# Attention rows and router logits from one matmul, the slot table entered two chunks after places, 16 instead of 40 warming matmuls

## The chip, the cores and the metric

One NeuronCore of a Trainium2 chip runs the whole program. The metric is the device time of one launch in microseconds (us). Matmuls run on TensorE (PE), with the load of their stationary operand shown apart as PEld; VectorE is DVE, ScalarE is ACT, GpSimd is POOL, and SyncE (SP) only starts DMAs here. Each engine takes its own instructions strictly in the written order and waits on semaphores for the others.

## The reference

Eight batches of 576 tokens pass three layers, all in float32. B=8, H=8, S=576, D=64, E=8.

```python
scores = q @ k.T / sqrt(64)              # per batch and head
ret = scores * where(i >= j, gamma[h] ** (i - j), 0)
x = (ret @ v)                            # 4608 tokens x 512
logits = x @ w_gate                      # 512 x 8
expert = argmax(logits)
gate = softmax(logits)[expert]
x = gate * (relu(x @ w1[expert]) @ w2[expert])     # 512 -> 1024 -> 512
h = x @ w_in                             # 512 -> 2048
out = (h * cos(h)) @ w_out               # 2048 -> 512
```

## The kernel before

The program has three stages, one after the other: attention with routing (0 to about 285 us in the profile), the experts (to 759 us, where the dense layer's first matmul starts) and the dense layer. The change lies in the first and at the seam to the second.

**Attention.** A batch's 576 tokens are five chunks of 128, 128, 128, 128 and 64; with eight batches that makes 40 chunks, and the loop over `i` runs 45 steps. Causal attention with decay is done as a recurrence: within a chunk by a masked score matrix (`scores`, `intra`), from earlier chunks by a 64x64 state per head that is kept in PSUM (tile `S`, copied to `sbd`) and multiplied with the queries (`inter`). A step holds pieces of several chunks: transposes of q and k of chunk i+1, scores of chunk i, output of chunk i-1, and the routing work of chunks i-2 and i-3. The schedule is written by hand: the order of the calls in the loop is the order on each engine, and no scheduler moves anything.

**Names.** `xt` holds a chunk's attention output with features on partitions; `rows` transposes it (tile `tp`) so that tokens lie on partitions, copies it to `xs` on ACT and stores it to `xd` in device memory, from where the experts later gather rows. `logits` multiplies `xt` by the router's weights (`wgp`, padded to 32 columns) into four 32-partition strips of `lg`; ACT copies them to `lt`; `logits_out` sums the strips and turns them over with a second matmul; DVE copies the eight logits of each token to `lgt`.

**Routing.** When a batch's logits are there, `route` finds the argmax (DVE), and `place` counts tokens before each one (short bf16 matmuls into `lg`) and works out each token's slot: a chain of some 15 small DVE instructions, one POOL instruction that DVE waits for, and more POOL instructions (`oh`, `rt`) behind it. `table` then enters token numbers and gates into the slot table with a matmul from `oh` and `rt`, and DVE adds the result to `tab`. Seven batches are placed as groups of five chunks; the last is split in groups of 2, 1 and 2 chunks, so that little is left at the end. After the last group `sid` (which row to gather for each slot) starts the gather DMAs of the first expert.

**PSUM.** There are eight banks of 128 x 512 float32. The attention stage uses two each for `tp`, `sc` (scores) and `x`, and one each for `S` and `lg`.

**The seam.** While the first gather runs, 40 bf16 matmuls whose result nobody reads are issued (`warm`, L189), so that PE is not idle. Behind them in PE's order stand the transposes of the first gathered rows (L602), which wait for the gate multiplication on ACT (L592), and then the experts' first layer (L620).

Of the kernel before, what the change touches and what calls it, by code (L numbers as in the profile page):

```python
# [11 lines left out]
F32 = mybir.dt.float32  # L12
# [5 lines left out]
ALU = mybir.AluOpType  # L18
AX = mybir.AxisListType
# [3 lines left out]
P = 128  # L23
# [3 lines left out]
E = 8  # L27
# [3 lines left out]
CH = [(0, 128), (128, 128), (256, 128), (384, 128), (512, 64)]  # L31
# [6 lines left out]
IDC = 2304  # L38
MAXOVB = 40
NWARM = 28  # L40
NWARM2 = 40
NWARM3 = 40

INV2PI = 1.0 / (2.0 * math.pi)
# [16 lines left out]
C_EYE = C_BASE + E  # L61
# [42 lines left out]
def attn_moe_kernel(ctx, tc, q, k, v, wg, w1, w2, win, wout, ctab, out):  # L104
    nc = tc.nc
# [3 lines left out]
    mm = nc.tensor.matmul  # L109
# [17 lines left out]
    ident = ct[:, C_ID:C_ID + 128]  # L127
# [54 lines left out]
    def w_units(e):  # L182
        return [(0, e, 0), (0, e, 1), (1, e, 0), (1, e, 1)]
# [8 lines left out]
    with ExitStack() as actx:  # L192
        ap1 = actx.enter_context(tc.tile_pool(name="ap1", bufs=1))
        ap2 = actx.enter_context(tc.tile_pool(name="ap2", bufs=2))
        ap3 = actx.enter_context(tc.tile_pool(name="ap3", bufs=3))
        ps2 = actx.enter_context(tc.tile_pool(name="ps2", bufs=2, space=PSUM))
        ps1 = actx.enter_context(tc.tile_pool(name="ps1", bufs=1, space=PSUM))
# [3 lines left out]
        def cc(col, n, rows=P):  # L201
            return ca[:rows, col - C_MASK:col - C_MASK + n]
# [4 lines left out]
        rsb = ap1.tile([P, E], BF16, name="rsb")  # L207
        rbase = ap1.tile([P, E], BF16, name="rbase")
        wgs = ap1.tile([P, 4, E], F32, name="wgs")
        wgp = ap1.tile([P, 4, 32], F32, name="wgp")  # L210
        nc.gpsimd.memset(wgp, 0.0)

        gx = ap1.tile([P, NCH, 4, P], F32, name="gx")
        tab = ap1.tile([P, 3, SL], F32, name="tab")
# [2 lines left out]
        def setup():  # L217
            nc.vector.tensor_copy(out=tri, in_=cc(C_TRI, P))
            nc.vector.tensor_copy(out=ones, in_=cc(C_ONE, P))
            nc.vector.tensor_copy(out=rbase, in_=cc(C_BASE, E))  # L220
            nc.vector.memset(rsb, 0.0)
            nc.vector.tensor_copy(out=wgp[:, :, 0:E], in_=wgs)

        def decay_table(c):
            for j in range(4):
# [3 lines left out]
        xts = []  # L229
        for i in range(3):  # L230
            t = ap1.tile([P, 4, P], F32, name=f"xt{i}")
# [3 lines left out]
        for i in range(2):  # L235
            t = ap1.tile([P, 4, P], F32, name=f"sbd{i}")
            nc.gpsimd.memset(t, 0.0)
            sbd.append(t)
        lgt = []
        for i in range(2):  # L240
            t = ap1.tile([P, NCH, E], F32, name=f"lgt{i}")
# [3 lines left out]
        steps = [(b, c) for b in range(B) for c in range(NCH)]  # L245
        NS = len(steps)
        st = [dict() for _ in steps]
# [35 lines left out]
        def scores(i):  # L283
            b, c = steps[i]
            o, n = CH[c]
            s = st[i]
            pT = ap2.tile([P, H, P], F32, tag="pT", name="pT")
            scs = [ps2.tile([P, 4, P], F32, tag="sc", name="sc") for g in range(2)]
            for a in range(4):
                for g in range(2):  # L290
                    r = 64 * g
                    mm(out=scs[g][:n, a, :n], lhsT=s["kpT"][r:r + 64, a, :n], rhs=s["qT"][r:r + 64, a, :n],
                       start=(a == 0), stop=True, skip_group_check=True)
            m = mask[:n, :n].unsqueeze(1).to_broadcast([n, 4, n])
            for g in range(2):
                nc.vector.tensor_mul(out=pT[:n, g::2, :n], in0=scs[g][:n, :, :n], in1=m)
            s["pT"] = pT
# [34 lines left out]
        def rows(i):  # L332
            b, c = steps[i]
            o, n = CH[c]
            pt = ps2.tile([P, 4, P], F32, tag="tp", name="tp")
            for j in range(4):
                nc.tensor.transpose(pt[:, j, :], xts[i % 3][:, j, :], ident)
            x = ap3.tile([P, 4, P], F32, tag="xs", name="xs")
            nc.scalar.copy(out=x[:n], in_=pt[:n])
            nc.sync.dma_start(out=xd[b * SEQ + o:b * SEQ + o + n, :], in_=x[:n].rearrange("p j t -> p (j t)"))  # L340

        def logits(i):
            b, c = steps[i]
            o, n = CH[c]
            s = st[i]
            x = xts[i % 3]
            lp = ps1.tile([P, 512], F32, tag="lg", name="lg")
            for j in range(4):
                mm(out=lp[32 * j:32 * j + 32, :n], lhsT=wgp[:, j, :], rhs=x[:, j, :n], start=True, stop=True,
                   skip_group_check=True)  # L350
            lt = ap2.tile([P, P], F32, tag="lt", name="lt")
            nc.scalar.copy(out=lt[:, :n], in_=lp[:, :n])
            s["lp"], s["lt"] = lp, lt

        def logits_out(i):
            b, c = steps[i]
            o, n = CH[c]
            s = st[i]
            lp, lt = s["lp"], s["lt"]
            mm(out=lp[:n, 256:256 + E], lhsT=lt[:, :n], rhs=cc(C_EYE, E), start=True, stop=True,  # L360
               skip_group_check=True)
            nc.vector.tensor_copy(out=lgt[b % 2][:n, c, :], in_=lp[:n, 256:256 + E])

        def cst(col, c0, n):
            return cc(col + c0 * E, n * E).rearrange("p (c e) -> p c e", e=E)
# [1 line left out]
        def route(i0, n):  # L367

            b, c0 = steps[i0]
            L = lgt[b % 2][:, c0:c0 + n, :]  # L370
            sh = [P, n, E]
            mx = ap2.tile([P, n], F32, tag="mx", name="mx")
            nc.vector.tensor_reduce(out=mx, in_=L, axis=AX.X, op=ALU.max)
            df = ap2.tile(sh, F32, tag="df", name="df", bufs=3)
            nc.vector.tensor_sub(out=df, in0=L, in1=mx.unsqueeze(2).to_broadcast(sh))
            sc = ap2.tile(sh, F32, tag="rsc", name="rsc")
            nc.vector.scalar_tensor_tensor(out=sc, in0=df, scalar=0.0, in1=cst(C_REV, c0, n), op0=ALU.is_ge,
                                           op1=ALU.mult)
            m2 = ap2.tile([P, n], F32, tag="m2", name="m2")
            nc.vector.tensor_reduce(out=m2, in_=sc, axis=AX.X, op=ALU.max)  # L380
            ohb = ap2.tile(sh, BF16, tag="ohb", name="ohb", bufs=3)
            nc.vector.tensor_tensor(out=ohb, in0=sc, in1=m2.unsqueeze(2).to_broadcast(sh), op=ALU.is_equal)
            routed.append((i0, n, ohb, df))
# [82 lines left out]
        def table(enter, gates):  # L466
            if gates is None:
                tp = enter(0, 3)
                nc.vector.tensor_add(out=tab, in0=tab, in1=tp)
                return  # L470
            tp = enter(0, 1)

            nc.vector.scalar_tensor_tensor(out=sid, in0=tab[:, 0, :], scalar=float(IDC), in1=tp[:, 0, :], op0=ALU.add,
                                           op1=ALU.add)
            gates()
            tp = enter(1, 3)
            nc.vector.tensor_add(out=tab[:, 1:3], in0=tab[:, 1:3], in1=tp)
            nc.vector.tensor_add(out=sgate, in0=tab[:, 1, :], in1=tab[:, 2, :])


        groups = {b * NCH + NCH - 1: (b * NCH, NCH) for b in range(B - 1)}
# [3 lines left out]
        routed = []  # L485
        tabled = []
# [20 lines left out]
        transposes(0)  # L507
        decay_k(1)
        wq = [(key, g) for key in w_units(0) for g in range(2)]
        for i in range(NS + 5):  # L510
            if i + 1 < NS:
                transposes(i + 1)
            if 0 <= i - 3 < NS:
                logits_out(i - 3)
            if i - 3 in groups:
                route(*groups[i - 3])
            if 0 <= i - 2 < NS:
                rows(i - 2)
            if i < NS:
                scores(i)  # L520
            if i + 2 < NS:
                decay_k(i + 2)
            if 20 <= i < 20 + len(wq):
                unit_split(*wq[i - 20], upA)
            if i == 0:
                setup()
            if 1 <= i <= NS:
                inter(i - 1)
                intra(i - 1)
            prev, tabled[:] = tabled[:], []  # L530
            for r in prev:
                table(*r)
            prev, routed[:] = routed[:], []
            for r in prev:
                place(*r)
            if 0 <= i - 2 < NS:
                logits(i - 2)
            if i + 4 < NS:
                loads(i + 4)
            if 18 <= i < 18 + len(wq):  # L540
                unit_load(ap3, *wq[i - 18])

        assert not tabled and not routed
        rp = ps2.tile([P, 512], F32, tag="x", name="xps")
        mm(out=rp[:, :E], lhsT=ones, rhs=rsb, start=True, stop=True)
        warm(NWARM2, ps2.tile([P, 512], F32, tag="x", name="xps"), ident)
        nc.vector.tensor_copy(out=cnt, in_=rp[:, :E])
# [3 lines left out]
        for e in range(1, E):  # L551
# [7 lines left out]
                                op=ALU.is_gt)  # L559
# [8 lines left out]
    with ExitStack() as mctx:  # L568
# [161 lines left out]
        pt = psX.tile([P, 4, P], F32, tag="tp", name="tp", bufs=2)  # L730
# [4 lines left out]
        for e in range(E):  # L735
# [5 lines left out]
            for i, (hf, l, k) in enumerate(work):  # L741
# [23 lines left out]
                if e + 1 < E:  # L765
                    if i % 3 == 0:
                        key = (w_units(e + 1)[i // 6], i // 3 % 2)
                        unit_load(stg, *key)
                        if i > 0:
                            j = i // 3 - 1  # L770
# [5 lines left out]
                if i == 1:  # L776
                    nc.sync.dma_start(out=idc[ds(at, NBLK * P), :].rearrange("(c p) o -> c (p o)", p=P),
                                      in_=sidT[e * NBLK:(e + 1) * NBLK, :])
# [270 lines left out]
```

## Time and profile before

| | us |
|---|---|
| median of 3 runs | 1559.72 (1557.36 to 1559.74) |
| the profiled execution | 1557.77 |
| its span | 1555.9 |
| PE busy | 1495.7 (96%) |
| DVE busy | 896.2 (58%) |
| ACT busy | 792.9 (51%) |
| POOL busy | 360.7 (23%) |

The profiled execution has 1.9 us outside its span. The busy shares are means over the three stages. In attention PE is the fullest engine as well, but it works through 3,086 short matmuls in the first 280 us, and what it waits for in each step must be read from the timeline. "Idle before" in brackets is the time that an engine waited just before the instruction, with the instruction that ended the wait.

### The profile page before, as it was taken

The page shows a single profiled execution, that of the slowest core. Times are in us where ns is not written, and L with a number is a line of the kernel's source. Part 1 is how long each engine was busy: PE and PEld are TensorE (multiplying, and loading weights), DVE is VectorE, ACT ScalarE, POOL GpSimd, SP SyncE. Part 2 cuts the span into 40 slices and gives each one's busy share as a digit, 9 for nine tenths or more (in the row PEclk, how much of TensorE's full clock was granted, in tenths as well). Part 3 has the DMA queues.
Part 4 walks back from the last instruction along what each step waited for, and adds up shares of the span by engine and source line. Part 5 has one row for each costly group of instructions (what it writes and reads, how often), then busy time and mean ns, then how long its engine had stood idle before and what let it go on. Part 6 is the DMA issues. An engine that isn't in the chain of part 4 may idle for free.

```text
span 1555.9 us, 25044 instructions
## 1 busy us (share of the span) xinstructions
PE 1495.7 (96%) x9829; PEld 1317.8 (85%) x9829; DVE 896.2 (58%) x1617; ACT 792.9 (51%) x1435; POOL 360.7 (23%) x400
## 2 busy tenths in 40 slices
PE   8998897899999999999999999999999999999998
PEld 6777776899999999999878888888888888888886
DVE  3556656547657656742266656666565656666554
ACT  3344433344444444342356666666665656666654
POOL 3112112456666666560000101010000101010101
PEclk9999998899999999999999999999999999999999
DMA  9668761456666656556630101000010100000000
GB/s 205 146 158 220 179 158 56 142 189 197 195 200 205 210 191 209 175 183 214 239 106 28 55 1 41 15 32 23 14 41 1 54 1 28 0 28 1 28 1 28
DMA packets 168523, 163.15 MB, mean 105 GB/s; under 512 B 119012, under 2 KB 127664, under 8 KB 166352
## 3 DMA queue, kind: packets, MB, share of 16 engines
q1 hardware_dynamic: 155696, 110.50, 25.5%
q0 software_dynamic: 10688, 36.31, 6.7%
q10 hardware_dynamic: 2016, 14.68, 2.8%
q8 instruction: 78, 1.28, 0.3%
q14 instruction: 45, 0.37, 0.1%
HBM read 115.70 MB, written 45.76 MB: 104 GB/s over the span
## 4 chain that ended last, share of the span: by engine, by line
issue 42%; PE 4%; POOL 2%; ACT 1%; DVE 1%; DMA 0%; POOLq 0%; SPq 0%
PE hps L921 2%; POOL out_dram L973 2%; PE acc L964 1%; PE acc L965 1%; PE acc L963 1%; DVE sa L932 0%; ACT ka L929 0%; DVE sa L933 0%; ACT sa L935 0%; ACT sa L936 0%; POOL spare L140 0%; DVE ka L931 0%; DMA yin<-ydT 0%; ACT sa L937 0%; DVE gl L948 0%
## 5 line engine op out<-in xcount | busy, mean ns | idle before, releaser
L921 PE MATMUL hps<-yT,wunit 128*128 128x512 f32 x1728 | 417.4, 391 | 0.4 <-ACT yT L908 0.4
L921 PEld LDWEIGHTS hps<-yT,wunit 128*128 128x128 f32 x1728 | 325.3, 189 | 69.3 <-ACT yT L908 1.1
L965 PE MATMUL acc<-wunit,gl 128*128 128x512 f32 x576 | 224.4, 390 | 0.0
L964 PE MATMUL acc<-wunit,gh 128*128 128x512 f32 x576 | 224.4, 390 | 0.0
L963 PE MATMUL acc<-wunit,gh 128*128 128x512 f32 x576 | 224.3, 389 | 0.0
L620 PE MATMUL hps<-xT,wunit 128*128 128x360 f32 (+1 forms) x1536 | 222.5, 306 | 0.8 <-ACT xT L605 0.6
L635 PE MATMUL hps<-hh,wunit 128*128 128x360 f32 (+1 forms) x1024 | 222.9, 309 | 0.0
L973 POOL DMA_INDIRECT out_dram<-orow,perm x36 | 35.2, 978 | 808.4 <-DVE orow L969 802.0
L620 PEld LDWEIGHTS hps<-xT,wunit 128*128 128x128 f32 x1536 | 220.3, 190 | 1.3 <-ACT xT L605 0.8
L943 DVE TENSOR_TENSOR sa<-hps,sa 128x512 f32<-128x512 f32 x144 | 99.4, 690 | 160.2 <-ACT sa L937 160.2
L935 ACT ACTIVATE sa<-sa 128x512 f32<-128x512 f32 x144 | 91.2, 633 | 193.7 <-DVE sa L933 193.7
L712 POOL TENSOR_TENSOR wunit<-wst,wunit 128x512 fp32r<-128x512 f32 x112 | 156.4, 1415 | 90.4 <-ACT wunit L711 89.7
L635 PEld LDWEIGHTS hps<-hh,wunit 128*128 128x128 f32 x1024 | 171.5, 192 | 0.0
L624 DVE SCALAR_TENSOR_TENSOR hl<-hps,hh 128x360 fp32r<-128x360 f32 (+1 forms) x128 | 60.6, 474 | 178.6 <-ACT hh L623 178.6
L635 PE MATMUL hps<-hl,wunit 128*128 128x360 f32 (+1 forms) x512 | 158.0, 309 | 4.8 <-DVE hl L624 4.8
L929 ACT ACTIVATE ka<-hps,biases 128x512 f32<-128x512 f32 x144 | 98.9, 687 | 69.2 <-PE hps L921 69.2
L963 PEld LDWEIGHTS acc<-wunit,gh 128*128 128x128 f32 x576 | 108.2, 188 | 22.5
L964 PEld LDWEIGHTS acc<-wunit,gh 128*128 128x128 f32 x576 | 108.3, 188 | 22.3
L965 PEld LDWEIGHTS acc<-wunit,gl 128*128 128x128 f32 x576 | 108.2, 188 | 22.3
L637 ACT COPY yev<-hps 128x256 f32<-128x256 f32 (+1 forms) x64 | 26.7, 417 | 168.5 <-issue 88.8
L937 ACT ACTIVATE sa<-sa,biases 128x512 f32<-128x512 f32 x144 | 104.2, 724 | 4.7
L931 DVE TENSOR_SCALAR ka<-ka 128x512 f32<-128x512 f32 x144 | 61.1, 424 | 73.9 <-ACT ka L929 73.9
(153 smaller groups left out, 2049.8 us busy)
## 6 DMA issues: line engine op xcount, KB each, us to landing
wst<-in_moe_w_dram SPq DMA_DIRECT2D x64, 512.0 KB, 4.7
wd<-cvo POOLq DMA_DIRECT2D x32, 512.0 KB, 3.8
wunit<-wd ACTq DMA_DIRECT2D x14, 1024.0 KB, 7.2
yin<-ydT SPq DMA_DIRECT2D x36, 256.0 KB, 2.7
ldq<-in_q_dram SPq DMA_DIRECT2D x32, 256.0 KB, 4.5
ldk<-in_k_dram SPq DMA_DIRECT2D x32, 256.0 KB, 4.6
ldv<-in_v_dram SPq DMA_DIRECT2D x32, 256.0 KB, 4.7
xd<-xs SPq DMA_DIRECT2D x32, 256.0 KB, 2.2
```

The lines of the kernel that those rows point to most:

```text
L620: mm(out=ph[:, :n], lhsT=u[:, a, kc, f0:f0 + P], rhs=t[:, bq, kc, :n], start=(idx == 0), stop=(idx == 11))
L635: mm(out=py[:, :n], lhsT=u[:, w], rhs=t[:, :n], start=(fc == 0 and g == 0), stop=(fc == 7 and g == 2))
L712: nc.gpsimd.tensor_sub(out=u[:, 1, 2 * g + c], in0=s[:, c], in1=u[:, 0, 2 * g + c])
L921: mm(out=ph, lhsT=u[:, a, kc, f0:f0 + P], rhs=t[:, bq, kc, :], start=(idx == 0), stop=(idx == 11))
L929: nc.scalar.activation(out=ka, in_=ph, func=AF.Identity, scale=INV2PI, bias=magic)
L935: nc.scalar.activation(out=sa, in_=sa, func=AF.Sin, scale=0.5)
L937: nc.scalar.activation(out=sa, in_=sa, func=AF.Identity, scale=-2.0, bias=one)
L943: nc.vector.tensor_mul(out=sa, in0=ph, in1=sa)
L963: mm(out=a, lhsT=gh[:, s], rhs=u[:, 0, fc % 4], start=(fc == 0), stop=False)
L964: mm(out=a, lhsT=gh[:, s], rhs=u[:, 1, fc % 4], start=False, stop=False)
L965: mm(out=a, lhsT=gl[:, s], rhs=u[:, 0, fc % 4], start=False, stop=(fc == 15))
L973: ins = nc.gpsimd.indirect_dma_start(out=out[:, :], out_offset=bass.IndirectOffsetOnAxis(ap=perm[:, k:k + 1], axis=0), in_=o, in_offset=None)
```

## The change

Three things are altered.

1. `rows` no longer transposes. It multiplies `xt` (stationary, 128 x 128) with a new table `wgi` that holds, for each of the four 128-feature blocks, an identity of 128 columns and the router's 8 weight columns. One matmul of 136 columns gives the block's rows and its part of the logits. ACT copies the rows to `xs`, and DVE adds the four parts of the logits straight into `lgt`. `logits`, `logits_out`, `lt` and their matmuls and copies are gone. The result needs two PSUM banks side by side, and these are the two that `scores` uses: both are now one tile of two banks, with one buffer.
2. `rows` and `route` stand at the end of a step, and `table` runs two steps after `place` instead of one (the last group: one).
3. `NWARM2` goes from 40 to 16.

```diff
-NWARM2 = 40
+NWARM2 = 16
...
+        RW = P + E
+        wgi = ap1.tile([P, 4, RW], F32, name="wgi")
...
-            nc.vector.tensor_copy(out=wgp[:, :, 0:E], in_=wgs)
+            nc.vector.tensor_copy(out=wgi[:, :, 0:P], in_=ident.unsqueeze(1).to_broadcast([P, 4, P]))
+            nc.vector.tensor_copy(out=wgi[:, :, P:RW], in_=wgs)
...
-            scs = [ps2.tile([P, 4, P], F32, tag="sc", name="sc") for g in range(2)]
+            two = ps1.tile([P, 8, P], F32, tag="sc", name="sc")
+            scs = [two[:, 0:4], two[:, 4:8]]
...
-            pt = ps2.tile([P, 4, P], F32, tag="tp", name="tp")
+            two = ps1.tile([P, 8, P], F32, tag="sc", name="rw").rearrange("p (j a) t -> p j (a t)", a=2)
             for j in range(4):
-                nc.tensor.transpose(pt[:, j, :], xts[i % 3][:, j, :], ident)
+                mm(out=two[:, j, 0:RW], lhsT=xts[i % 3][:, j, :], rhs=wgi[:, j, :], start=(j % 2 == 0), stop=True,
+                   skip_group_check=True)
             x = ap3.tile([P, 4, P], F32, tag="xs", name="xs")
-            nc.scalar.copy(out=x[:n], in_=pt[:n])
+            nc.scalar.copy(out=x[:n], in_=two[:n, :, 0:P])
+            nc.vector.tensor_reduce(out=lgt[b % 2][:n, c, :], in_=two[:n, :, P:RW].rearrange("p j e -> p e j"),
+                                    axis=AX.X, op=ALU.add)
...
-            if 0 <= i - 3 < NS:
-                logits_out(i - 3)
-            if i - 3 in groups:
-                route(*groups[i - 3])
-            if 0 <= i - 2 < NS:
-                rows(i - 2)
             if i < NS:
                 scores(i)
...
-            prev, tabled[:] = tabled[:], []
+            prev, waiting[:], tabled[:] = waiting[:], tabled[:], []
             for r in prev:
                 table(*r)
+            if i >= NS + 2:
+                while waiting:
+                    table(*waiting.pop(0))
             prev, routed[:] = routed[:], []
             for r in prev:
                 place(*r)
             if 0 <= i - 2 < NS:
-                logits(i - 2)
+                rows(i - 2)
+            if i - 2 in groups:
+                route(*groups[i - 2])
```

On PE, from the end of a place (the matmuls with `ones` and `ohb`) to the next scores, this stood before (`xt_126` and `xt_128` are buffers of `xt`, `wgp` the router's weights, `ct` the identity):

```order
L400 MATMUL lg<-ohb,ones 128x8
L349 MATMUL lg<-xt_126,wgp 32x128 [waits DVE_49]
L349 MATMUL lg<-xt_126,wgp 32x128 x3
L277 MATMUL tp<-ct,ldq 128x64 [waits DMAHW3_49,Activation_49]
L277 MATMUL tp<-ct,kp 128x64 [waits Activation_49]
L360 MATMUL lg<-ca,lt 128x8 [waits Activation_49]
L337 MATMUL tp<-ct,xt_128 128x128 [waits Activation_49]
L292 MATMUL sc<-qT,kpT 128x128 x8
```

At the same place it is now (`rw` is the two-bank tile of rows and logits):

```order
L384 MATMUL lg<-ohb,ones 128x8
L340 MATMUL rw<-wgi,xt_125 128x136 [waits DVE_49,PE_49]
L340 MATMUL rw<-wgi,xt_125 128x136 x3
L279 MATMUL tp<-ct,ldq 128x64 [waits DMAHW3_49,Activation_49]
L279 MATMUL tp<-ct,kp 128x64 [waits DVE_49,Activation_49]
L295 MATMUL sc<-qT,kpT 128x128 [waits DVE_49]
L295 MATMUL sc<-qT,kpT 128x128 x7
```

The three pieces of logits and rows have become one, and the scores, which waited for nothing, now wait for a DVE instruction.

On DVE, the end of a place and what follows it, before (`rsb` is the last result of `place`):

```order
L453 CAST rsb<-rsum 128x8 [waits DVE_49]
L362 COPY lgt_136<-lg 128x8 [waits PE_49]
L296 TENSOR_TENSOR pT<-sc,ca 128x4x128 [waits PE_49] x2
L267 TENSOR_TENSOR kp<-ldk,ca 128x512 [waits DMAHW1_49]
L322 TENSOR_TENSOR xt_126<-xps,gx 128x512 [waits PE_49]
```

And now:

```order
L437 CAST rsb<-rsum 128x8 [waits DVE_49]
L344 TENSOR_REDUCE lgt_135<-rw 128x8 [waits Activation_49]
L299 TENSOR_TENSOR pT<-sc,ca 128x4x128 [waits PE_49]
L299 TENSOR_TENSOR pT<-sc,ca 128x4x128
L269 TENSOR_TENSOR kp<-ldk,ca 128x512 [waits DMAHW1_49]
L325 TENSOR_TENSOR xt_127<-xps,gx 128x512 [waits PE_49]
```

The reduction that empties `rw` waits for ACT's copy out of the same banks and stands behind all of the place's DVE instructions.

## Rows read from the trace of the kernel before

**Rows 1.** What PE waited for, 20 to 244 us: total, times, longest.

```profile
PE lg L460 <- POOL rt L440: 9.6, 6, 2.4
PE lg L349 <- DVE t L404: 3.1, 6, 1.0
PE tp L337 <- DVE lgt L362: 2.4, 4, 0.8
PE lg L349 <- DVE tab L469: 2.2, 6, 0.4
PE tp L337 <- ACT qT L280: 2.1, 11, 0.5
```

**Rows 2.** Timeline of PE: start, duration, instructions, idle before.

```profile
233.46 0.66 PE L277 MATMUL tp<-ct,ldq 128*128 128x128 f32 x4
...
234.39 0.29 PE L360 MATMUL lg<-ca,lt 128*128 128x8 f32 x2
...
243.98 0.19 PE L392 MATMUL lg<-rbase,ones 128*128 128x40 bf16 x1
...
244.60 0.42 PE L349 MATMUL lg<-xt,wgp 128*32 128x128 f32 x8 [0.29 <-DVE t L404]
244.96 0.47 PE L277 MATMUL tp<-ct,ldq 64*128 64x64 f32 x4
...
245.60 0.39 PE L360 MATMUL lg<-ca,lt 128*128 128x8 f32 x2
245.88 0.66 PE L337 MATMUL tp<-ct,xt 128*128 128x128 f32 x4
246.47 1.16 PE L292 MATMUL sc<-qT,kpT 64*128 64x128 f32 x16
247.56 1.16 PE L310 MATMUL xps<-qT,sbd 128*128 128x128 f32 x8
248.65 1.09 PE L320 MATMUL xps<-pT,ldv 128*64 128x128 f32 x16
```

**Rows 3.** Timeline of DVE around the place at 244 us.

```profile
239.80 0.20 DVE L373 TENSOR_REDUCE mx<-lgt 128x5 f32<-128x40 f32 x1
...
244.35 0.20 DVE L404 TENSOR_TENSOR t<-lg,ohb 128x40 f32<-128x40 f32 x1
...
248.77 0.16 DVE L362 COPY lgt<-lg 128x8 f32<-128x8 f32 x1
```

**Rows 4.** Timeline of ACT, the copy of a chunk's rows.

```profile
246.58 0.58 ACT L339 COPY xs<-tp 128x512 f32<-128x512 f32 x1 [0.47 <-PE tp L337]
```

**Rows 5.** Windows: length, busy of PE, PEld, DVE, ACT, POOL; granted clock, DMA share, GB/s.

```profile
63.00:71.00 8.00, 8.00 (x74) 7.21 (x78) 2.15 (x5) 1.93 (x4) 0.00 (x0) 0.57 0.59 126
159.00:163.00 4.00, 3.96 (x34) 3.44 (x36) 0.17 (x1) 1.87 (x4) 0.00 (x0) 0.57 0.27 104
262.00:275.00 13.00, 5.79 (x37) 4.05 (x37) 8.28 (x48) 1.45 (x5) 2.49 (x7) 0.50 0.19 55
804.00:808.00 4.00, 4.00 (x11) 3.11 (x11) 0.80 (x2) 0.89 (x2) 0.00 (x0) 0.57 0.00 0
```

**Rows 6.** Timeline of PE in the dense layer, a wait.

```profile
803.63 0.25 PE L991 MATMUL hps<-ct,permf 36*128 36x36 f32 x1 [2.07 <-DVE permf L989]
```

**Rows 7.** Timeline of DVE, first instruction of two of the last places.

```profile
257.86 0.17 DVE L404 TENSOR_TENSOR t<-lg,ohb 128x16 f32<-128x16 f32 x1
...
270.07 0.17 DVE L404 TENSOR_TENSOR t<-lg,ohb 128x16 f32<-128x16 f32 x1 [0.29 <-PE lg L400]
```

**Rows 8.** Timeline of all engines at the seam to the experts.

```profile
275.44 6.18 PE L189 MATMUL xps<-ct 128*128 128x256 bf16 x40
...
278.12 0.72 ACT L592 ACTIVATE xrow<-xrow,sgate 128x512 f32<-128x512 f32 x1 [8.71 <-DMA xrow<-xd,sid]
...
281.72 0.63 PE L602 MATMUL tp<-ct,xrow 128*128 128x128 f32 x4
...
285.02 0.51 PE L620 MATMUL hps<-xT,wunit 128*128 128x256 f32 x2 [0.57 <-ACT xT L605]
```

More of the change, by code (lines that the diff above doesn't have):

```diff
@@ L209, in attn_moe_kernel @@
         wgs = ap1.tile([P, 4, E], F32, name="wgs")
-        wgp = ap1.tile([P, 4, 32], F32, name="wgp")
-        nc.gpsimd.memset(wgp, 0.0)
+        RW = P + E
+        wgi = ap1.tile([P, 4, RW], F32, name="wgi")
         gx = ap1.tile([P, NCH, 4, P], F32, name="gx")
@@ L334, in rows @@
             o, n = CH[c]
-            pt = ps2.tile([P, 4, P], F32, tag="tp", name="tp")
+            two = ps1.tile([P, 8, P], F32, tag="sc", name="rw").rearrange("p (j a) t -> p j (a t)", a=2)
             for j in range(4):
-                nc.tensor.transpose(pt[:, j, :], xts[i % 3][:, j, :], ident)
+                mm(out=two[:, j, 0:RW], lhsT=xts[i % 3][:, j, :], rhs=wgi[:, j, :], start=(j % 2 == 0), stop=True,
+                   skip_group_check=True)
             x = ap3.tile([P, 4, P], F32, tag="xs", name="xs")
-            nc.scalar.copy(out=x[:n], in_=pt[:n])
+            nc.scalar.copy(out=x[:n], in_=two[:n, :, 0:P])
+            nc.vector.tensor_reduce(out=lgt[b % 2][:n, c, :], in_=two[:n, :, P:RW].rearrange("p j e -> p e j"),
+                                    axis=AX.X, op=ALU.add)
             nc.sync.dma_start(out=xd[b * SEQ + o:b * SEQ + o + n, :], in_=x[:n].rearrange("p j t -> p (j t)"))
[L342 to L362, printed above, removed]
         def cst(col, c0, n):
@@ L509, in attn_moe_kernel @@
         wq = [(key, g) for key in w_units(0) for g in range(2)]
+        waiting = []
         for i in range(NS + 5):
@@ L541, in attn_moe_kernel @@
                 unit_load(ap3, *wq[i - 18])
+        assert not tabled and not routed and not waiting
         assert not tabled and not routed
```

## The prediction, before the changed kernel was run

> **What bounds the kernel now.** I read the waits of PE over the attention stage first, then PE's and DVE's timelines around one place, and last the granted clock in windows. Between 20 and 244 us PE waits little: the five rows add up to 19.4 us, and half of it is `table` waiting for POOL's `rt`, six times with 2.4 us as the longest [rows 1]. In between PE's instructions follow each other without a gap [rows 2]: the stage goes at PE's pace, and whatever is taken from PE or made to wait on PE shows in the time. A place occupies DVE from 244.35 to 248.77 [rows 3], and nothing on PE waits for its end: the scores start at 246.47, in the middle of it [rows 2]. That is the cover which the change removes. The granted clock is 1.0 for most of the stage; it fell to 0.5 twice in it, around 64 to 70 us and 159 to 163 us, and stays there at its end [rows 5]. At the seam, the transposes of the first gathered rows start at 281.72, right where the warming matmuls end (275.44 + 6.18), while the gate multiplication that they need ended at 278.12 + 0.72 = 278.84 [rows 8].
>
> **The work on PE.** Per chunk the old way costs the logits 0.36 (244.60 to 244.96), the sum over strips 0.28 to 0.39 (245.60) and the transposes 0.59 (245.88 to 246.47): 1.23 to 1.34 [rows 2]. The new matmul is not in the trace. The nearest row is `inter`: four float32 matmuls with 128 x 128 weights, shown as eight passes, 1.09 from start to start and 1.16 as recorded (247.56, 248.65) [rows 2]; the new one is alike with 136 columns for 128. At worst it costs 1.16 and saves 0.1, at best 1.09 and saves 0.25; I take 0.2, which for the 35 chunks done up to 244 us is -7.0. The transposes alone are 0.59 against 1.09 for the matmul with an identity. The Trainium skill, Perfetto Trace Analysis, Transposes, says to use the transpose rather than a plain matmul for such work, as it skips the arithmetic; by it this exchange would be a loss of 0.5 a chunk, and the rows agree on that half. What turns it into a gain is the 0.64 to 0.75 of logits work that goes away.
>
> **Waits that go.** The rows that wait for POOL's `rt` (9.6), for `tab` (2.2) and for `t` (3.1) belong to the single `lg` buffer and to the table one step after the place; in the new order the table stands a whole step of PE's work (over 4 us) later, where POOL was 2.4 late at most, and the logits no longer use `lg`. The waits of the old transposes for `lgt` and `qT` (2.4 and 2.1) came from a third user of the two `tp` buffers. All 19.4 go [rows 1]: -19.4, at least if nothing takes their place.
>
> **The new wait.** `rw` and the scores share one tile now, so the scores of step i+1 wait until ACT has copied the rows and DVE has reduced the logits, in this order, as the change's rows show. In an ordinary step that chain is 0.11 from the matmul's end to ACT (246.47 to 246.58) and 0.58 for the copy [rows 4], about 0.2 for the reduction (0.20 for one of 40 columns [rows 3]; the new one reads 32) and some 0.1 for two hand-overs: 0.98. On PE the next chunk's transposes lie beside it, 0.93 for full chunks (233.46 to 234.39) [rows 2]. So 0.05 is left, and 0.3 where the chunk has 64 tokens (244.96 to 245.60 is 0.64): 1.5 in all.
>
> In the step after a place the reduction is queued behind the place. With the place's first matmul at time 0 (243.98), DVE comes free at 4.79 (248.77) [rows 2, 3]; the reduction and the hand-over make it 5.05. PE has finished the place at 0.33, the rows' matmul at 1.45 and the short transposes at 2.1. It then waits 2.95 us for its scores, and behind them in PE's queue stands everything else. Six such waits lie before 244 us: +17.7. In steps 20 to 27 DVE also splits weights; before, this made the copy to `lgt` late by 2.4 in all [rows 1], now it makes the reduction as late and starts two places later: +3.4.
>
> Sum up to 244 us: -7.0 - 19.4 + 17.7 + 3.4 + 1.5 = -3.8.
>
> **The end of attention.** From the last full place (243.98) to the next group's place (257.86) before were 13.9 us, from there to the last place (270.07) 12.2 [rows 2, 7]. Walking the new order with the same durations: the scores of step 38 start at 5.05, those of step 39 at 10.8 (here no transposes cover the chain), table and place follow, and DVE begins the second group at 15.5: +1.6. After it each rows' matmul waits for the reduction before it, which stands behind a place on DVE, and the last group's place waits for the table of the one before: 11.7 instead of 12.2, if PE's clock is full. It was at 0.50 from 262 to 275 [rows 5]; then one matmul that nothing covers takes 1.1 more. So +1.1 to +2.2; I take +2.0. What follows the last place is unaltered.
>
> **The clock.** In the two stretches of attention at 0.57 mean, 8 x 0.43 = 3.4 us and 4 x 0.43 = 1.7 us of PE's time were lost, 5.1 together [rows 5]. The second fall came after the wait of 2.4, and the wait of 2.07 in the dense layer was followed by a fall as well (803.63, then 0.57 from 804 to 808) [rows 1, 5, 6]; of the six waits for `rt`, mostly 1.4, only one more was. Waits of 2.95 are longer than both. I count six falls among the seven waits of the new order, at the smaller price, since dense matmuls follow: 6 x 1.7 = 10.2, less the 5.1 that go: +5.1. The ends are none (-5.1) and seven at 3.4 (+18.7).
>
> **The seam.** A matmul of 256 columns takes 0.21 at 1.2 GHz and 0.11 at 2.4, if a column goes in at each pulse (an estimate; 16 and 24 of these make 6.0, and the 40 took 6.18 [rows 8]). 16 at the lower clock are 3.4 and end at 278.85, just when the gate multiplication ends (278.84). The transposes can start 2.8 us sooner, and so does the first layer, now at 285.02 [rows 8]: -2.8. Everything behind it is PE's. If the lower clock holds longer for the lack of matmuls, nothing of it is left: 0.
>
> **Sum.** -3.8 + 2.0 + 5.1 - 2.8 = +0.5 on the profiled execution's 1557.77 (span 1555.9 and 1.9 around it): 1558.3. The median of the runs lies 1.95 above that execution, so 1560.2.
>
> **Rivals.**
> (1) The clock stays up through the new waits. For it: most waits of 1.4 left it at 1.0. Against it: both waits above 2 us. Then -5.1 instead of +5.1: 1550.
> (2) The falls cost more than they did before. After each of the seven waits PE goes at 0.5 for as long as around 64 to 70 us in half of them, 2.55 on average, 17.9: +12.8 instead of +5.1, 1568. For it: the falls come at every batch, and the first of the old ones cost 3.4. Against it: what follows the new wait is scores, `inter` and `intra`, the densest part of a step. It decides from about eight us of lost clock on; below that the forecast holds.
> (3) The chain is bare in every step: ACT or DVE come to `rw` so late that the transposes don't cover it. Each of 39 steps then loses up to 0.93: +36, 1596. The Trainium skill, Perfetto Trace Analysis, Matmuls, says that independent groups should rotate through PSUM banks so that one's evacuation overlaps the next one's matmuls, and one buffer for rows and scores is against that rule. Against it here: the 0.93 of transposes write to `tp` [rows 2], and in the step of 246 us ACT began its copy 0.11 after the last matmul, so that it was not late [rows 4].
>
> **How the numbers follow.** No change (the forecast): 0.41. Faster by rival 1, or by fewer falls and a cheaper matmul: 0.27. Slower by rival 2, or by a seam that gives nothing: 0.29; rival 3: 0.03. About 0.2% (3.1 us) is what a measurement of this kernel can tell from no change. The forecast's own range is 1556.6 to 1563; from rival 1 to rival 2 it is 1550 to 1568, and I set 1551 to 1568. Faster 0.27, same 0.41, slower 0.32.
>
> **What would show it.** In the new profile PE should wait for DVE's reduction before the scores about 2.9 us, seven times, and nearly nothing for `rt`, `tab` and `t`; the eight passes of the new matmul should take 1.1; the stretches with a clock of 0.5 in attention should be about six, right after those waits; the experts' first layer should start 12.2 us after the last place's first DVE instruction instead of 15.0 (285.02 - 270.07) [rows 7, 8]. The forecast is wrong if the clock's stretches are none or twice as long, or if the scores wait in ordinary steps too.

## The result, and the profile after

| | before | after |
|---|---|---|
| median of the runs, us | 1558.54 (1555.99 to 1559.74, 4 runs) | 1570.30 (1567.64 to 1571.70, 4 runs) |
| span of the profiled execution, us | 1555.9 | 1569.8 |
| its mean granted clock | 0.983 | 0.971 |

The ratio is 1.0076, interval 1.0056 to 1.0095. The change makes the kernel 11.8 us slower. The forecast was 1560 and no change; the time lies 2.3 us above the range.

The waits of PE in the changed kernel, from 20 us to the last full place (waited for, total, times, longest):

```profile
PE sc L295 <- DVE lgt L344: 25.4, 11, 3.7
```

The five rows of [rows 1] are gone and one has taken their place: the scores wait for DVE's reduction of the logits. One such wait, on PE (start, duration, instructions, idle before):

```profile
224.61 0.41 PE L279 MATMUL tp<-ct,kp 64*128 64x64 f32 x4
228.04 2.08 PE L295 MATMUL sc<-qT,kpT 64*128 64x128 f32 x16 [3.03 <-DVE lgt L344]
230.05 1.83 PE L313 MATMUL xps<-qT,sbd 128*128 128x128 f32 x8
```

And DVE at the same place:

```profile
223.38 0.20 DVE L388 TENSOR_TENSOR t<-lg,ohb 128x40 f32<-128x40 f32 x1
...
227.72 0.17 DVE L437 CAST rsb<-rsum 128x8 bf16<-128x8 f32 x1
227.81 0.18 DVE L344 TENSOR_REDUCE lgt<-rw 128x8 f32<-128x32 f32 x1
```

The place keeps DVE from 223.38 to 227.81; only then does the reduction empty the tile that the scores need. There are seven such waits, 3.02 to 3.05 each, six in the row above and the seventh at 259.79 us. The scores behind this one take 2.08 and `inter` 1.83, where they took 1.16 each before [rows 2]: the granted clock has fallen to half (called a fall from here on). Seven of the ten stretches of the changed kernel (length, PE, PEld, DVE, ACT, POOL busy, PEclk, DMA share, GB/s), against [rows 5]:

```profile
57.00:61.00 4.00, 3.89 (x26) 3.44 (x28) 1.95 (x4) 0.00 (x0) 2.48 (x5) 0.57 0.72 138
88.00:95.00 7.00, 6.12 (x48) 5.67 (x50) 2.69 (x10) 0.00 (x0) 3.25 (x6) 0.51 0.51 104
149.00:153.00 4.00, 4.00 (x42) 3.77 (x40) 3.52 (x5) 1.05 (x1) 0.00 (x0) 0.57 1.07 227
184.00:190.00 6.00, 4.94 (x34) 4.50 (x36) 4.82 (x12) 2.33 (x4) 0.00 (x0) 0.50 0.80 163
228.00:232.00 4.00, 3.96 (x28) 3.61 (x30) 1.84 (x3) 0.00 (x0) 2.41 (x5) 0.57 0.69 129
259.00:265.00 6.00, 5.21 (x36) 4.76 (x38) 1.92 (x7) 0.00 (x0) 3.16 (x6) 0.50 0.00 0
279.00:300.00 21.00, 11.44 (x49) 8.50 (x49) 11.36 (x60) 3.89 (x7) 6.87 (x11) 0.51 0.47 143
```

Read in windows of 1 us, PE was at 0.5 of its clock (1.2 GHz) nine times between 20 and 266 us: six times for 3.4 us (57, 122, 149, 159, 197, 228) and three times for 6.8 (88, 183, 258), 40.8 in all. Before, it was 6.8 and 3.4 up to 244 us, 10.2 in all. Seven of the nine come with the waits after the places; the other two come with two waits in steps 20 to 27, which split the experts' weights (scores at 147.88 after 2.59, and at 185.06 after 3.71).

The long falls differ from the short ones in where they begin. In the changed kernel the six of 3.4 us began when PE was at work again, up to 1.7 us after the wait; the three of 6.8 us began 0.7 to 1.4 us before the wait was over. Two stretches show it, one after the wait that ended at 147.88 and one inside the wait that ended at 185.06 (columns as above):

```profile
148.00:149.00 1.00, 1.00 (x17) 0.88 (x17) 0.86 (x5) 0.11 (x1) 0.00 (x0) 1.00 0.68 164
184.00:185.00 1.00, 0.00 (x0) 0.00 (x0) 1.00 (x3) 1.00 (x3) 0.00 (x0) 0.50 0.14 43
```

The two weight-step waits begin on ACT, here in the changed kernel:

```profile
144.84 1.04 ACT L179 CAST wunit<-wst 128x1024 fp32r<-128x1024 f32 x1 [3.95 <-DMA wst<-in_moe_w_dram]
...
146.57 0.58 ACT L343 COPY xs<-rw 64x512 f32<-64x512 f32 x1
```

ACT stands still for weights that have not landed, and the copy of the rows queues behind it. This happens six times, 14.2 us in all; before, no cast waited. SP's queue of the changed kernel shows the reason, with ACT's copy that the first store waits for:

```profile
128.31 0.59 ACT L343 COPY xs<-rw 128x512 f32<-128x512 f32 x1 [0.30 <-PE rw L340]
...
128.93 0.34 SPq L346 DMA_DIRECT2D xd<-xs  x1
129.36 0.39 SPq L256 DMA_DIRECT2D ldq<-in_q_dram  x1
...
131.26 2.63 SPq L171 DMA_DIRECT2D wst<-in_moe_w_dram  x1
```

The same load, the first of the weights, in the kernel before:

```profile
123.67 0.89 SPq L171 DMA_DIRECT2D wst<-in_moe_w_dram  x1
```

The store of the rows waits for ACT's copy, which now comes at the end of a step, and everything behind it on SP's queue, this load too, is issued later: at 131.26 instead of 123.67.

The seam, PE in the changed kernel, against [rows 8]:

```profile
290.81 3.58 PE L189 MATMUL xps<-ct 128*128 128x256 bf16 x16
294.49 1.09 PE L588 MATMUL tp<-ct,xrow 128*128 128x128 f32 x4
...
298.66 1.73 PE L606 MATMUL hps<-xT,wunit 128*128 128x256 f32 x5 [0.46 <-ACT xT L591]
```

From the last place's first DVE instruction (285.44) to the first layer are 13.2 us; 12.2 was forecast and 15.0 was before. The transposes still go at 1.2 GHz.

The spans of the two profiled executions differ by 13.9 us, more than the medians, since the changed kernel's is the slowest of its four. By stretches between the same instructions: to the first place -1.5; from there to the third +1.1; to the fifth, where the weights are split, +9.1; to the seventh +2.1; to the last place +4.6; to the first expert matmul -1.7; the rest +0.3.

### The profile page after: what moved, and what is told of

It is laid out like the page before. It is cut to its first block, busy times and chain, and to the rows that moved or that the text cites. A ratio compares the mean times of both kernels' runs of the same rounds, so it can differ in the third digit from the quotient of the medians.

```text
span 1569.8 us, 24472 instructions
## 1 busy us (share of the span) xinstructions
PE 1502.7 (96%) x9565; PEld 1334.4 (85%) x9565; DVE 896.1 (57%) x1618; ACT 781.1 (50%) x1395; POOL 359.3 (23%) x399
## 4 chain that ended last, share of the span: by engine, by line
issue 42%; PE 4%; POOL 2%; ACT 1%; DVE 1%; DMA 0%; POOLq 0%; SPq 0%
PE hps L907 2%; POOL out_dram L959 2%; PE acc L949 1%; PE acc L951 1%; PE acc L950 1%; DVE sa L918 0%; ACT ka L915 0%; DVE sa L919 0%; ACT sa L921 0%; ACT sa L922 0%; POOL spare L140 0%; DVE ka L917 0%; DMA yin<-ydT 0%; ACT sa L923 0%; DVE gl L934 0%
```

## The experiments

Each result is the median in us and its ratio to the kernel before, with the 95% interval. Each time stands beside runs of the kernel before on the same chip; their medians were 1558.6, 1558.1, 1559.9 and 1557.7 in the four sets.

**1. `rows_first`.** The rows go ahead of the place, so that DVE empties their tile first.

```diff
+            if 0 <= i - 2 < NS:
+                rows(i - 2)
             prev, routed[:] = routed[:], []
...
-            if 0 <= i - 2 < NS:
-                rows(i - 2)
```

> The changed kernel with one thing moved: in a step that has a place, the rows' matmul with its copy and reduction is written ahead of the place. Theory A (the scores wait because the reduction is queued behind the place on DVE, and each such wait drops the clock): the seven waits of 3.0 us (21 us) and the time lost to the lower clock behind them (7 stretches, 1.7 to 3.4 each, some 14 us) go; 30 to 37 us less than the changed kernel, so 1534 to 1540, faster than the kernel before too. Rival B (the shared two-bank tile costs in every step, or the loads bound the stage): the seven waits go but others take their place, 1560 or more.

1553.95, ratio 0.9972 (0.9957 to 0.9987): neither of the two. The scores after a place no longer waited 3 us, but the profile shows a second wait of the same tile (waits of PE, 20 to 250 us):

```profile
PE rw L340 <- DVE pT L299: 13.8, 7, 2.0
PE sc L295 <- DVE lgt L344: 7.1, 8, 2.9
```

The next rows' matmul needs the tile back from the scores, and the mask `pT` that empties it stands behind the place, DVE in this kernel:

```profile
88.25 0.17 DVE L437 CAST rsb<-rsum 128x8 bf16<-128x8 f32 x1
88.33 1.28 DVE L299 TENSOR_TENSOR pT<-sc,ca 128x512 f32<-128x512 f32 x2
```

So a place on DVE stops PE from either side, 3.0 us or 2.0.

**2. `loads_first`.** SP issues the store of the rows behind the loads of the step (`store` is the store cut out of `rows`).

```diff
                 unit_load(ap3, *wq[i - 18])
+            if 0 <= i - 2 < NS:
+                store(i - 2)
```

> The changed kernel with the store of the rows issued behind the loads and the weight load of its step instead of ahead of them on SP's queue. Theory C (SP waits at the store for ACT's copy at a step's end, so every load is issued later than before, and the expert weights land late in steps 20 to 27): the two waits of 2.6 and 3.7 us and the small ones before them (7 us) go with the two falls of the clock behind them (about 4 us): 8 to 12 less than the changed kernel, 1558 to 1562. Rival D (the DMA engines are simply full in that stretch, their share is 1.0): the weights land late all the same, less than 2 us gained.

1565.03, ratio 1.0043 (1.0025 to 1.0061): 5.3 less than the change, against 8 to 12. No cast waits for its weights any more, and of the 7.0 us in these steps 0.6 are left. The first weight load in this kernel, 131.26 in the changed one:

```profile
121.65 0.92 SPq L171 DMA_DIRECT2D wst<-in_moe_w_dram  x1
```

But two of the places' waits are now 3.7, since the weights' split on DVE stands in front of the place, and the clock still fell with all seven, four times for 6.8 us. C has the mechanism and overrates it.

**3. `both`.** Edits 1 and 2.

> Both moves together. By A and C the gains add: 40 to 48 less than the changed kernel, 1522 to 1530. If both waits cover the same time, or if the faster stage runs into the loads, little more than the larger one: 1534 to 1540.

1550.37, ratio 0.9954 (0.9934 to 0.9974). The rows' matmul still waits 13.8 for `pT`, as in experiment 1, and the scores 2.2 in 7. That is above both ranges: of the seven waits for `pT`, 1.96 to 1.99 us each, five were followed by a fall.

**4. `fill`.** 20 matmuls on PE in the step after a place, between the transposes and the scores.

```diff
+            if filled and i < NS:
+                warm(20, ps2.tile([P, 512], F32, tag="tp", name="fill"), ident)
             if i < NS:
                 scores(i)
...
+            filled = bool(prev)
```

> The changed kernel with 20 bf16 matmuls of 256 columns, whose result is not used, in each of the seven waits after a place (between the transposes and the scores). The waits stay, since the scores still need DVE's reduction. Theory A1 (the falls of the clock are a cost of their own): the granted clock stays at 1.0 in the step after each place and 10 to 14 us go: 1556 to 1560. Rival A2 (at the lower clock the step is no longer than what DVE and ACT need anyway): the clock stays up and the time does not move by more than 3 us.

1554.57, ratio 0.9975 (0.9961 to 0.9989): 15.7 us less than the change with the waits as long as they were. PE in this kernel:

```profile
114.87 2.34 PE L189 MATMUL fill<-ct 128*128 128x256 bf16 x20 [0.35 <-ACT qT L282]
117.55 1.16 PE L295 MATMUL sc<-qT,kpT 64*128 64x128 f32 x16 [0.34 <-DVE lgt L344]
```

0.35 + 2.34 + 0.34 is the 3.03 of the changed kernel, filled with work that computes nothing, and the scores take 1.16 instead of the 1.74 of the changed kernel at this place. Between 20 and 250 us the clock fell once, after a wait in a weight step. So the falls are a cost of their own, as A1 has it, and more than its 10 to 14 went; covering them gives back more than the change had lost (11.8). The 15.7 are not the places' falls alone: in this profile, whose time is 1551.23, the waits in the weight steps are 4.7 us instead of 7.0 as well (2.47, 1.58, and 0.7 on top of a filled one), and one of the two falls behind them is gone.

**5. `table_late`.** The kernel before with the table two steps after its place, and nothing else.

```diff
-            prev, tabled[:] = tabled[:], []
+            prev, waiting[:], tabled[:] = waiting[:], tabled[:], []
             for r in prev:
                 table(*r)
+            if i >= NS + 2:
+                while waiting:
+                    table(*waiting.pop(0))
```

> The kernel before, with nothing changed but the table, which is entered two steps after its place instead of one. Theory T (the table's waits cost what they showed): the six waits of the table for POOL's rt (9.6 us, the longest 2.4), the one for tab (2.2) and that for t (3.1) go, and the fall of the clock that followed one of them (1.7) too; nothing takes their place, since the logits keep their own tile. 1542 to 1549. Rival U: those waits covered something that stays (the logits matmul in the single lg buffer, which the table also uses), so that others wait instead: less than 4 us gained, 1555 to 1559.

1544.59, ratio 0.9918 (0.9904 to 0.9932): -13.5, theory T. The 9.6 for POOL's `rt` are gone; those for `tab` and `t` stayed (2.2 and 3.4 up to 240 us), where T had them go, and the clock did not fall from 22 to 245 us.

**6. `warm16`.** The kernel before with `NWARM2 = 16`.

> The kernel before, with 16 warming matmuls ahead of the gathered rows in place of 40. Theory V (as predicted): the transposes of the gathered rows start 1.8 to 2.8 us sooner, 1556 to 1557. Rival W: without these matmuls the lower clock holds longer into the experts' first layer, at 1.2 for 2.4 GHz, and the gain is lost: 1558 to 1560.

1552.93, ratio 0.9968 (0.9956 to 0.9981): -5.2, more than either said. In its profile the fall at 63 us of the kernel before is missing as well, so that the size is not the seam's alone; the pairs of 9 and 12 are the better measure.

**7. `split`.** On `both`: the second half of a place on DVE (the block's row, gates, counts) a step later.

```diff
+            if last:
+                place2(i0, n, ohb, ex, dd, hot, True, tabled)
+            else:
+                half.append((i0, n, ohb, ex, dd, hot, False, waiting))
...
             if 0 <= i - 2 < NS:
                 rows(i - 2)
+            prev, half[:] = half[:], []
+            for r in prev:
+                place2(*r)
```

> On the kernel both (rows ahead of the place, loads ahead of the store): VectorE's work for a place is cut in two. The part from the ranks to the one-hot of the slot blocks stays; the block's row, the gates and the running counts (2.4 us of VectorE) come one step later, behind that step's reduction, and the table two steps after the place as now. Theory X (all that is left of the loss in both is pT queued behind a place, and the clock that falls after it): the seven waits of 2.0 us of the rows' matmul shrink below 0.5 and the clock falls at most twice before the tail: 11 us of waits and some 8 to 10 of clock, 1528 to 1541. Rival Y: the work only moves, and the scores of the step after wait for the reduction or the table for POOL's one-hot rows, by as much: 1548 to 1552.

1551.32, ratio 0.9964 (0.9947 to 0.9980): rival Y. The wait for `pT` is gone, and the table waits instead. PE in this kernel:

```profile
94.43 1.24 PE L459 MATMUL lg<-rt,oh 128*128 128x120 f32 x5 [2.04 <-POOL rt L439]
```

And POOL in the same stretch of it:

```profile
89.44 3.97 POOL L425 TENSOR_SCALAR oh<-ca,rm 128x128 fp32r<-128x128 f32 x5 [2.52 <-DVE gts L431]
93.38 0.52 POOL L439 TENSOR_TENSOR rt<-hot,gh 128x200 fp32r<-128x200 f32 x1
93.86 0.52 POOL L439 TENSOR_TENSOR rt<-hot,gl 128x200 fp32r<-128x200 f32 x1
```

POOL starts its one-hot rows as the second half begins, and ends 4.9 us later, when the table stands at PE already.

**8. `split3`.** As 7, the table one step later still.

```diff
-                half.append((i0, n, ohb, ex, dd, hot, False, waiting))
+                half.append((i0, n, ohb, ex, dd, hot, False, tabled))
```

> As split, with the table three steps after the place. In split the rows' matmul no longer waited for pT, but the table waited for POOL's rt, 16.6 us in 8, the longest 3.2, since POOL now begins its one-hot rows a step later. Theory X: with one more step between, those waits go and nothing follows them: 14 us of waits and the falls of the clock after them, 1530 to 1540. Rival Y: another wait takes their place again (the next rows' matmul, the scores, or the lg buffer): 1546 to 1553.

1528.54, ratio 0.9799 (0.9787 to 0.9812): theory X, and 31 us below the kernel before. Its waits of PE, 20 to 225 us:

```profile
PE sc L295 <- DVE lgt L344: 2.1, 6, 0.9
```

And stretches of it (columns as above):

```profile
60.00:120.00 60.00, 59.38 (x772) 53.65 (x774) 37.81 (x107) 23.31 (x55) 18.69 (x27) 1.00 0.82 185
120.00:180.00 60.00, 58.85 (x755) 53.21 (x754) 45.32 (x105) 29.34 (x58) 14.87 (x20) 1.00 1.00 232
234.00:252.00 18.00, 9.06 (x42) 7.07 (x41) 11.81 (x68) 1.52 (x3) 6.62 (x13) 0.53 0.31 91
```

PE is busy 59 of 60 us at a clock of 1.00 up to the tail, still with one tile for rows and scores. The first layer starts at 254.76 (285.02 before).

**9. `late16`.** Edits 5 and 6 on the kernel before.

> The kernel before with the table two steps after its place and with 16 warming matmuls; logits, their sum and the transposes of the rows stay as they were. The two gains add if they touch different stretches: 1544.6 less the 2.8 to 5.2 of the 16 matmuls, 1539 to 1542. If the 5.2 of the 16 matmuls was a clock that held in attention by chance, 1541.5 to 1544.

1541.30, ratio 0.9878 (0.9862 to 0.9895): 3.3 below `table_late`, or 5.1 if each is taken against its own runs of the kernel before. It is the fastest that was measured of the old structure, on which a place cut in two was not tried; `split3` lies 12.8 below it.

**10. `fill_loads`** was meant to be 4 with 2, but its store stood behind `route` and still ahead of the loads:

```diff
             if i - 2 in groups:
                 route(*groups[i - 2])
+            if 0 <= i - 2 < NS:
+                store(i - 2)
             if i + 4 < NS:
                 loads(i + 4)
```

> The changed kernel with both repairs that were measured apart: 20 matmuls on PE before the scores in the step after a place (1554.6 alone) and the store issued behind the loads on SP's queue (5 us less alone). Theory A (the loss is the clock after the waits, plus the late weight loads): the weight-split waits (8.3 us with the matmuls alone) fall to about 2 and the falls of the clock that they caused go, 1546 to 1550. Rival D (the loads were late for the DMA traffic, not for the store): 1553 to 1556.

1551.11, ratio 0.9951 (0.9935 to 0.9967). It decides nothing between A and D. It shows that `fill` repeats within 3.5 us, and that behind the store the weights are late here too (13.5 in 7).

**11. `fill_loads2`.** As 10, with the store behind `unit_load`.

> As fill_loads was meant to be: 20 matmuls before the scores in the step after a place, and the store of the rows issued behind the loads of the same step. In fill_loads the store still stood ahead of the loads, so its order of transfers was that of fill, and its casts waited for the expert weights like those (13.5 us in 7). Theory A (the store ahead of the loads makes the weights late): no cast waits for its weights, no fall of the clock before the tail, and 4 to 8 us less than fill's 1551 to 1555: 1545 to 1549. Rival D (the DMA traffic makes them late): the casts wait as before, 1551 to 1555.

1548.37, ratio 0.9940 (0.9928 to 0.9952): theory A. What shows it is the profile, in which no cast waits and the clock did not fall from 20 to 255 us; it is that of the fastest execution, 1544.09. The time alone would not: it is 2.7 below `fill_loads`, and the intervals overlap. The waits of PE up to 240 us:

```profile
PE sc L295 <- DVE lgt L344: 4.6, 10, 1.0
PE fill L189 <- ACT qT L282: 2.5, 7, 0.4
```

With the filling matmuls still on PE, 21.9 us of the change's time are gone; since the scores still wait for the places as long as before, that is clock and late weights.

**12. `warm40`.** The changed kernel with `NWARM2 = 40`.

> The changed kernel with 40 warming matmuls at the seam, as before the change. Theory V (the seam gains by the 24 matmuls left out, less the lower clock behind them): 1.7 to 3.3 us slower than the changed kernel's 1570.3, 1572 to 1574. Rival W (with 40 the clock comes back sooner, and the first layer gets back what the wait cost): 1568.5 to 1570.5.

1572.47, ratio 1.0093 (1.0079 to 1.0108): 2.2 above the change, theory V. The first layer starts 10.1 us after the warming matmuls begin (289.57 to 299.63), 7.85 with 16 (290.81 to 298.66), and in the latter it runs at 1.2 GHz until 303.2. With 40 the clock came back sooner, by 295, but fell again from 300.9 to 304.3; W is right on the clock and wrong on the gain.

## Why the prediction was wrong

**Right.** The mechanism of the change: the scores wait behind the place on DVE, 3.02 to 3.05 each against 2.95, and in ordinary steps the transposes cover the chain, so rival 3 did not come. The new matmul takes 1.00 to 1.12 from start to start at the full clock against 1.1. The waits of [rows 1] went, and `table_late` shows that the delayed table alone is worth 13.5. Exchanging transposes for matmuls with an identity was no loss by these rows, 1.00 to 1.12 against 1.23 to 1.34, since the logits' matmuls go with them. No run isolates it: `split3` lies 12.8 below `late16`, but it also lacks the waits of the logits' pieces, has its places cut in two, and enters the table another step later. The Trainium skill, Perfetto Trace Analysis, Transposes, wants a transpose rather than a standard matmul; for that pair alone the rows agree (0.59 against 1.00 to 1.12), for the whole exchange they do not.

**The clock: +5.1 forecast, at most +15.3 measured.** This is the failed step: "I count six falls among the seven waits of the new order, at the smaller price". All seven waits came with a fall, two of them for 6.8 us, and two more falls came in the weight steps. 40.8 us at half the clock cost a busy PE 20.4, less the 5.1 of before; PE was idle in 3.1 of the 40.8, which makes it some +13.8 rather than +15.3. The smaller price was chosen with the reason that dense matmuls follow; the same dense scores and `inter` follow all of the waits, and the long falls began before these were released. Rival 2 had the mechanism, and 17.9 for the seven waits against at most 15.3 (30.6 us at half the clock); the other two falls, at most 5.1, it did not have. The prediction's own upper end, seven at 3.4 (+18.7), would have covered this; the top of its range was set by rival 2 (+12.8). `fill` shows by experiment that the falls cost time: cover the places' waits, and 15.7 us go, some of it in the weight steps.

**Steps 20 to 27: +3.4 forecast, 7.0 measured, and their two falls on top.** The failed step is "now it makes the reduction as late": it took the lateness of the old copy over as it was. The change moves the rows, and with them the store, to the end of a step, and SP's queue has the next loads and the weights behind that store. The prediction did not follow the store on SP; so the casts that wait (14.2 us), the copies behind them, and the scores behind these were not in the sum. `loads_first` and `fill_loads2` show that it is the order on SP's queue: with the store behind the loads no cast waits, though the DMA share is about as high (0.88 in `loads_first` and 0.87 in `fill_loads2` from 120 to 190 us, 0.85 in the changed kernel). The Trainium skill, Perfetto Trace Analysis, DMA Optimizations, says that it may make sense to give loads and stores to different engines; no run here did that, and the order on the one queue was enough to end the casts' waits.

**End of attention: +2.0 forecast, +4.6 measured.** The fall at the last full place (6.8 us from 258.8, PE idle in the first 1.0) is about 2.9 of it; without it the walk gave 1.7.

**Seam: -2.8 forecast, -1.7 measured**, since the transposes and the start of the first layer remain at 1.2 GHz; `warm40` gives 2.2 and `late16` 3.3 for the same 24 matmuls.

Together, up to the seventh place: -3.8 and +5.1 of clock were forecast, +1.3 (the end's fall counted in it); measured are +10.8, 9.5 more. Of these the clock explains at most 6.8 (34.0 us at half, 17.0, less 5.1, instead of 5.1; 5.8 without the 2.1 us in which PE was idle) and the late weights 3.6. The work and the other waits came out as forecast, or up to 0.9 better.

What stays open: why a fall lasts 3.4 us in one place and 6.8 in another. In the changed kernel, `loads_first`, `warm40`, `rows_first` and `both` all thirteen falls of 6.8 us from 20 to 262 us held 0.6 to 1.5 us in which PE still or again stood idle, and the twenty of 3.4 us under 0.2. That is not all of it: two falls of 6.8 us in `split` (125 and 190 us) and the one in the kernel before (64 us) held none, and no run moved the moment on purpose.

## What to carry to other kernels

When two stages come to share a buffer, write down for each engine what stands ahead of the instruction that empties it: here a place of 4.4 us on DVE, which stopped PE before the scores or, with the order turned round, before the next rows, until it was cut in two and the table entered a step later. Move a step, and follow its DMA issues too: a store that waits on its queue delays every load behind it. And a wait on PE is to be priced twice, its own length and the slow clock after it: with the same waits filled with matmuls whose result nobody reads, the kernel took 15.7 us less.

## What the runs showed of the hardware

- PE's clock at a wait. All nine waits of 2.5 us and more in the changed kernel came with 3.4 or 6.8 us at 1.2 GHz. Of the seven waits of 1.96 to 1.99 in `rows_first` two did (119 and 248 us), of the seven in `both` five, of the five of 2.04 to 2.06 in `split` four. The falls at waits of 2 us differ from place to place with the same work around them.
- Short waits mostly left the clock up, not always. In `split3`, `table_late` and `fill_loads2`, with waits up to 1.1, it did not fall between 22 and 234 us; in `late16`, with nearly the same waits as `table_late`, it fell for 3.4 us at 176, two us after a wait of 0.97, and in `warm16` at 150 after one of 0.97.
- Filling a wait with matmuls whose result nobody reads kept the clock, 20 of 256 columns (2.34 us) for a wait of 3.03: in `fill`, `fill_loads` and `fill_loads2` none of the 21 filled waits came with a fall. It doesn't shorten the wait.
